# Layer 1's softmax in two passes of four heads, in a two-layer decode kernel

## The chip, the cores and the metric

The kernel runs on one NeuronCore of a Trainium2 chip. Its engines have queues of their own and run side by side: TensorE (PE, with weight loads PEld), VectorE (DVE), ScalarE (ACT), GpSimd (POOL) and the queue that issues transfers (SP), served by 16 DMA engines. The metric is the device time in microseconds (us) of the whole program. The kernel before takes 230.61 us, the median of three runs (230.2, 230.61 and 233.4).

## What is computed

Two layers, each of them an attention with residual and a feed-forward with residual, over 8 batch rows of one token each. Both layers use the same weights and the same K and V caches.

```python
def _A_ref(x, k_cache, v_cache, wq, wo):            # x: 8 x 1 x 448
    W = 1024                                        # the last 1024 of 4096 positions
    q = (x @ wq) -> 16 heads of 256
    k = repeat(k_cache[:, :, Sk - W:, :], 2)        # 8 KV heads, two query heads each
    v = repeat(v_cache[:, :, Sk - W:, :], 2)
    p = softmax(q . k * 256 ** -0.5)
    return (p . v) @ wo                             # 4096 -> 448
def _B_ref(x, w1, w2): return silu(x @ w1) @ w2     # 448 -> 1792 -> 448

x = A_x
x = x + A(layernorm(x)); x = x + B(layernorm(x))    # layer 1
x = x + A(layernorm(x)); x = x + B(layernorm(x))    # layer 2
```

A batch row needs 8 KV heads of K and of V, 512 KB each, so 16 loads or 8.4 MB a row and 67 MB in all; the weights add 10 MB. Everything is bfloat16 in HBM.

## The kernel before

**Rows and slots.** The work goes row by row, `b` = 0 to 7. The loads `K0..K7, V0..V7` of each row are issued in that order on the SP queue (`load_kv`, L496) into a ring of `R = 30` slots. A load may be issued when the load 30 places before it in the ring has been used for the last time. K head `k` of a row is last read by layer 2's scores of that row, V head `k` by layer 2's value products. Counting the ring round, the last two V loads of row `b+1` (`V6`, `V7`) and `K0`, `K1` of row `b+2` take the slots of `K0..K3` of row `b`, which layer 2's scores of heads 0 to 3 read (named `S1.0` below). `K2..K5` of row `b+2` wait for the scores of heads 4 to 7 (`S1.1`), the others for the value products of layer 2 (`PV1`).

**One row.** K heads are transposed in place by VectorE (L639; heads 0 to 3 in one piece, `KW`, 1.2 us, heads 4 to 7 in two pieces, `KT`, 0.68 us each). Layer 1: the scores of heads 0 to 3 (`S0.0`) and then of heads 4 to 7 (`S0.1`), both L656, both in the PSUM bank `SC[0]`, in rows 0 to 15 of each quarter of 32 partitions: `S0.0` fills 16 rows and `S0.1` rewrites 8 of them. One softmax (`softmax`) then covers all heads: negated maximum (`max`, L673, VectorE), a small masked copy (`mq`, L674, ScalarE), a matmul that spreads it (`mx`, L675), the bias (`mb`, L677), the exponentials (`exp`, L688, ScalarE), a permutation (`perm`, L690), a transpose (`turn`, L692), the sums (`l`, L694) and their reciprocal (`rl`, L697). The value products of heads 0 to 5 (`PV0`, L703, four matmuls of 512 columns a head) go to bank `OB[0]`; the last `LATE = 2` heads (`products_late`, named `PV6` and `PV7`, L712, eight matmuls of 256 columns a head) go to the free half of `SC[0]`. `o_turn` scales (`oev`, L725), transposes (`oT`, L729) and evicts (`oTev`, L733); `wo_rows` multiplies by `wo` (L754); `fold` brings the sum of one row into columns (`rowb`, L760, then L529 and L532).

**The chain of a row.** `chain(b)` then runs layer 1's feed-forward and layer 2's query: `xb1` (L765), statistics (L771 to L776), `w1a`, `w1b` (L544) with their turns `w1T` (L549), `tanh` (L798), `hT` (L806), `w2` (L818), `rowb2`, `fold2`, `xb2`, `wq0` and `wq1` (L833) with their turns `qT` (L838), the masked queries `qm0`, `qm1` (L839), the query expansion `qx` (L846) and its eviction `qbd` (L850). After that come `S1.0`, `S1.1`, a softmax and `PV1` of layer 2. The last row's layer 2 is cut in two halves; layer 2's end of rows 0 to 6 is done for all of them at once (`final_rows`), beside the last row's chain, and the last row ends in `final_last`.

**Order.** The order of the tasks on each engine is written out by hand in `ORDER`, as numbers of tasks. The engines wait by semaphores; a dependence is made wherever a task reads or writes what another wrote or read. So a task of one row that stands behind a task of the next row on VectorE waits for it, whatever it needs itself. In row 6, for instance, VectorE has (row in brackets):

```
KW0[7] KW1[7] xb1[6] KW2[7] w1Tb[6] w1Ta[6] rl1[5] hTb[6] hTa[6] KW3[7] KT4[7] KT5[7] xb2[6] KT5[7] KT6[7]
qT0a[6] qT0b[6] qm0[6] KT4[7] qT1[6] qm1[6] KT7[7] KT6[7] KT7[7] max1[6] max0[7] ...
```

TensorE has extra matmuls (`warm`, named `fill`, L781) between its tasks, whose results nobody reads.

Of the kernel before, what the change touches and what calls it, by code (L numbers as in the profile page):

```python
# [36 lines left out]
    "dve":  # L37
# [14 lines left out]
    "act":  # L52
# [8 lines left out]
    "pool":  # L61
        "0 1 79 130 131 239 269 270 256 404 403 373 390 536 506 523 537 669 639 656 670 802 772 789 803 905 935 936 "
        "922 1068 1069 1038 1055 1156 1173 1210 1273",
# [160 lines left out]
def bass_interleave_layers__sliding_block_cached__dense_activation_silu__decode_kernel(  # L224
# [20 lines left out]
    LATE = 2  # L245
# [416 lines left out]
    def softmax(b, L, part=None):  # L662

        sb, n, m = (SC[L], L, L) if part is None else (part[0], part[1], 1 - part[1])
        lb = bank[LB[n]]
        x = bank[sb][:, 0:256]
        px = lb[:, 256:512]
        mneg, bias, acc, rlr = (sm[b][:, 4 * n + i:4 * n + i + 1] for i in range(4))
        mq = sm[b][:, 8 + 4 * n:12 + 4 * n]
        K = [("sm", b, n, i) for i in range(5)]  # L670
        mx, lr = lb[:, C_MX:C_MX + 4], lb[:, C_L:C_L + 1]
        if part is None:
            dve(lambda e: e.tensor_reduce(mneg, x, AX.X, ALU.max, negate=True), bk(sb), [K[0]], 0.41, b, "max%d" % L)  # L673
            act(lambda e: e.activation(mq, sel4, ACTF.Copy, scale=mneg), [K[0], "sel4"], [K[4]], 0.2, b, "mq%d" % L)  # L674
            pe(lambda e: e.matmul(mx, quad[:], mq, start=True, stop=True, skip_group_check=True), [K[4], "quad"],  # L675
               bk(LB[n]), 0.2, b, "mx%d" % L)
            dve(lambda e: e.tensor_reduce(bias, mx, AX.X, ALU.min), bk(LB[n]), [K[1]], 0.15, b, "mb%d" % L)  # L677
        else:
            mt, mg = part[2][:, 0:64].bitcast(F32), part[2][:, 64:80].bitcast(F32)
            bias = mt[:, 0:1]  # L680
            dve(lambda e: e.tensor_reduce(mt[:, 0:1], x, AX.X, ALU.max, negate=True), bk(sb), [("mt", n)] + part[3], 0.41,
                b, "max%d" % L)
            dve(lambda e: e.transpose(mt, mt), [("mt", n)], [("mt", n)], 0.21, b, "mT")
            dve(lambda e: e.tensor_reduce(mg, mt.rearrange("p (n q) -> p n q", q=4), AX.X, ALU.min), [("mt", n)],
                [("mg", n)] + part[3], 0.17, b, "mg")
            dve(lambda e: e.transpose(mt.rearrange("p (n q) -> p n q", q=4), mg.unsqueeze(2).broadcast_to([P, 8, 4])),
                [("mg", n)], [("mt", n), K[1]], 0.21, b, "mb")
        act(lambda e: e.activation(e_sb[m], x, ACTF.Exp, bias=bias, scale=1.0, accum_out=acc),  # L688
            bk(sb) + [K[1]], EK[m] + [K[2]], 0.6, b, "exp%d" % L)
        pe(lambda e: e.matmul(px, perm[:], e_sb[m], start=True, stop=True),  # L690
# [408 lines left out]
```

## Time and profile before

| | |
|---|---|
| times of three runs | 230.2, 230.61, 233.4 us |
| the profiled execution | 230.15 us, its span 228.4 us |
| busy share of the span | PE 76%, DVE 69%, PEld 41%, ACT 31%, POOL 10% |
| granted TensorE clock | 1.000 |
| DMA | 78.21 MB, mean 342 GB/s over the span |
| costliest group | L639 transposes of K on DVE, 96 instructions, 80.2 us |
| scores | L656, 1024 matmuls, 40.9 us |
| value products | L703, 416 matmuls, 31.1 us; L712, 192 matmuls, 8.6 us |

The span lies 1.75 us under the time of the same execution; a sum made on the trace is therefore set against 230.15 us, and that execution stands 0.46 us under the median of the runs. "Busy" of PE counts the modelled end of each pipelined matmul, so a busy PE is not a full one. The DMA share is the mean over the 16 engines of the time that packets took; a little over 1 means that packets overlap.

### The profile page before, as it was taken

The numbers are of one execution on the slowest core, as the hardware profiler recorded it, in microseconds if no ns is written. First come the engines' busy times: TensorE is split into PE (matmuls) and PEld (weight loads), VectorE is DVE, ScalarE is ACT, GpSimd is POOL, SyncE is SP. The second block draws the span as 40 slices with busy tenths as digits, with TensorE's granted clock in tenths as the row PEclk, the third lists the DMA queues.
The fourth block names the chain that finished last, engine by engine and source line by source line (L and its number), as shares of the span: only waits on it lengthen the run. The fifth ranks groups of instructions, "written<-read, shape, count | busy, mean of one in ns | idle before, by whom it ended". The sixth has DMA issues, their size and how long they took to land.

```text
span 228.4 us, 8452 instructions
## 1 busy us (share of the span) xinstructions
PE 173.0 (76%) x3779; PEld 94.1 (41%) x3779; DVE 157.2 (69%) x369; ACT 71.4 (31%) x218; POOL 22.8 (10%) x41
## 2 busy tenths in 40 slices
PE   0020737357878989999898987888989999999894
PEld 0010623123444455445444644554445445544662
DVE  6238989878792797389459837974895589314644
ACT  2000080633302341432324142414332431353341
POOL 1000130000200210101010101110120200000020
PEclk9999999999999999999999999999999999999999
DMA  6999999999999999999999999999999999700000
GB/s 175 413 406 407 382 380 395 411 414 417 405 400 369 377 408 403 396 408 407 406 406 408 402 378 411 408 392 395 410 409 385 380 408 406 307 3 3 0 6 1
DMA packets 22681, 78.21 MB, mean 342 GB/s; under 512 B 2279, under 2 KB 5302, under 8 KB 22262
## 3 DMA queue, kind: packets, MB, share of 16 engines
q1 hardware_dynamic: 22486, 77.32, 86.6%
q8 instruction: 29, 0.48, 0.9%
q10 hardware_dynamic: 160, 0.36, 0.6%
q14 instruction: 6, 0.05, 0.1%
HBM read 77.67 MB, written 0.01 MB: 340 GB/s over the span
## 4 chain that ended last, share of the span: by engine, by line
PE 46%; DVE 31%; DMA 10%; ACT 6%; issue 4%; SPq 2%; DVEq 0%; ACTq 0%
DVE slot L639 12%; DMA slot<-in_A_k_cache_dram 10%; PE bank L656 10%; PE bank L703 7%; DVE slot L472 7%; PE pair L754 6%; PE bank L781 2%; PE pair L833 2%; ACT ot L760 2%; PE bank L675 2%; PE bank L846 2%; PE bank L712 2%; PE bank L833 2%; PE pair L529 2%; PE pair L818 1%
## 5 line engine op out<-in xcount | busy, mean ns | idle before, releaser
L639 DVE STREAM_TRANSPOSE slot<-slot 128x512 uint32<-128x512 uint32 (+1 forms) x96 | 80.2, 866 | 7.0 <-DMA slot<-in_A_k_cache_dram 6.8
L656 PE MATMUL bank<-slot,qbd 128*16 128x256 bf16 (+1 forms) x1024 | 40.9, 285 | 5.1 <-DVE slot L639 2.0
L703 PE MATMUL bank<-slot,qbd 128*24 128x512 bf16 (+6 forms) x416 | 31.1, 393 | 3.5 <-DVE qbd L692 3.3
L656 PEld LDWEIGHTS bank<-slot,qbd 128*16 128x16 bf16 (+1 forms) x1024 | 23.2, 87 | 16.7 <-ACT qbd L850 4.0
L781 PE MATMUL bank<-wq_sb,cols 128*1 128x512 bf16 x192 | 19.6, 416 | 13.9 <-DMA wq_sb<-in_A_wq_dram 13.9
L776 POOL TENSOR_TENSOR fcols<-fcols 128x1 f32<-128x1 f32 x17 | 9.4, 554 | 106.4 <-ACT fcols L774 94.5
L754 PE MATMUL pair<-wo_sb,q1s 128*1 128x449 bf16 x288 | 17.2, 353 | 1.1 <-DVE wo_sb L475 0.8
L850 ACT ACTIVATE qbd<-bank 128x256 bf16<-128x256 f32 x16 | 6.1, 384 | 33.5 <-PE bank L846 33.5
L725 ACT ACTIVATE ot<-bank,q1s 128x512 bf16<-128x512 f32 (+1 forms) x16 | 10.8, 673 | 16.4 <-PE bank L703 11.1
L626 POOL TENSOR_TENSOR qbd<-q1s,fcols 128x256 bf16<-128x256 bf16 x16 | 9.7, 614 | 59.7 <-PE bank L712 42.4
L703 PEld LDWEIGHTS bank<-slot,qbd 128*24 128x24 bf16 (+6 forms) x416 | 9.7, 92 | 11.1 <-DVE qbd L692 4.2
L692 DVE STREAM_TRANSPOSE qbd<-bank 128x256 bf16<-128x256 bf16 x17 | 8.0, 473 | 8.2 <-PE bank L690 7.9
L673 DVE TENSOR_REDUCE q1s<-bank 128x1 f32<-128x256 f32 x15 | 6.3, 423 | 8.1 <-PE bank L656 8.0
L472 DVE TENSOR_REDUCE slot<-wo_sb 128x6 f32<-128x2688 bf16 x4 | 11.8, 2948 | 0.1
L781 PEld LDWEIGHTS bank<-wq_sb,cols 128*1 128x1 bf16 x192 | 4.2, 82 | 15.4 <-issue 13.9
L674 ACT ACTIVATE q1s<-fcols,q1s 128x4 f32<-128x4 f32 x15 | 4.4, 296 | 18.7 <-DVE q1s L673 18.7
L675 PE MATMUL bank<-q1s,quad 128*128 128x4 f32 x30 | 6.0, 269 | 4.7 <-ACT q1s L674 4.5
L598 PE MATMUL pair<-slot,wq_sb 128*128 128x16 bf16 x128 | 3.6, 174 | 7.5 <-DVE slot L591 7.5
L833 PE MATMUL pair<-wq_sb,q1s 128*1 128x256 bf16 x256 | 8.9, 275 | 0.3 <-DVE q1s L765 0.3
L688 ACT ACTIVATE qbd<-bank,q1s 128x256 bf16<-128x256 f32 x15 | 7.1, 472 | 6.3 <-DVE q1s L677 6.0
L712 PE MATMUL bank<-slot,qbd 128*7 128x256 bf16 (+7 forms) x192 | 8.6, 283 | 0.6 <-DVE qbd L692 0.6
L833 PE MATMUL bank<-wq_sb,q1s 128*1 128x512 bf16 x128 | 8.8, 390 | 0.0
(168 smaller groups left out, 244.6 us busy)
## 6 DMA issues: line engine op xcount, KB each, us to landing
slot<-in_A_k_cache_dram SPq DMA_DIRECT2D x64, 512.0 KB, 8.3
slot<-in_A_v_cache_dram SPq DMA_DIRECT2D x64, 512.0 KB, 10.1
wo_sb<-in_A_wo_dram SPq DMA_DIRECT2D x4, 896.0 KB, 14.6
wq_sb<-in_A_wq_dram SPq DMA_DIRECT2D x3, 1024.0 KB, 8.0
w_sb<-in_B_w_dram SPq DMA_DIRECT2D x1, 1568.0 KB, 19.8
w_sb<-in_B_w_dram SPq DMA_DIRECT2D x1, 1344.0 KB, 17.2
wq_sb<-in_A_wq_dram ACTq DMA_DIRECT2D x1, 256.0 KB, 3.5
wq_sb<-in_A_wq_dram SPq DMA_DIRECT2D x1, 256.0 KB, 4.1
```

The costliest lines, as they stand in the source:

```text
L472: dve(lambda e, rows=rows, s=s: e.tensor_reduce(s, rows[:, :, R0:M1].rearrange("p c (a n) -> p c a n", a=2), AX.X, ALU.add, negate=True), ...
L626: pool(lambda e, k2=k2: e.tensor_tensor(qdata(0, k2), q1s[:, b, 64 * k2:64 * k2 + 64].rearrange("p (n r) -> p n r", r=2).unsqueeze(3) .bro ...
L639: dve(lambda e, v=v: e.transpose(v, v), keys, keys, 0.15 + n / 2 / 950, b, ("KW%d" if n > 1024 else "KT%d") % k)
L656: fns.append(lambda e, w=w, j=j, kv=kv, cb=cb, par=par: e.matmul(sc[32 * j:32 * j + up_to, 0:256], w, kv, start=(cb == 0 and par == 0), st ...
L675: pe(lambda e: e.matmul(mx, quad[:], mq, start=True, stop=True, skip_group_check=True), [K[4], "quad"], bk(LB[n]), 0.2, b, "mx%d" % L)
L703: pe([lambda e, t=t: e.matmul(bank[ob][32 * t:32 * t + m, :], pT_sb[L][:, 64 * t:64 * t + m], v[:, 512 * t:512 * t + 512], start=True, sto ...
L712: pe([lambda e, t=t, a=a: e.matmul(o[32 * t:32 * t + m, :], pT_sb[n][:, 64 * t + a:64 * t + a + m], v[:, 512 * t + DH * a:512 * t + DH * a ...
L725: act(lambda e: e.activation(o_t, src[1], ACTF.Copy, scale=sm[b][:, 4 * L + 3:4 * L + 4]), bk(src[0]) + [("sm", b, L, 3)], okey, 0.62, b, ...
L754: fns.append(lambda e, i=i, w=w, c0=c0: e.matmul(bank[XB][32 * (i % 4):32 * (i % 4) + 1, c0:c0 + D + 1], oT[:, oT_col(i):oT_col(i) + 1], w ...
L776: pool(lambda e: e.tensor_tensor(rhalf, var4, nhalf, ALU.pow), ["var4", "nhalf"], ["rhalf"], 0.54, b, "pow" + name)
L781: pe([lambda e, i=i: e.matmul(bank[OB[0]][32 * i:32 * i + 1, :], zero_b, wq_sb[:, 512 * i:512 * i + 512], start=True, stop=True, tile_posi ...
L833: pe([lambda e, j=j, c=c, qh=qh, k2=k2, h=h, n=n: e.matmul(qh[32 * j:32 * j + 1, :], xbt[b][:, xcol(c, k2):xcol(c, k2) + 1], view(wq_sb[:] ...
```

## The change

Layer 1's softmax is called twice a row, with `g = 0` for heads 0 to 3 as soon as `S0.0` is done, and with `g = 1` for heads 4 to 7 after `S0.1`. The exponentials, and then the turned probabilities, of pass `g` are written over the block of masked queries that its scores have used. Pass 0 uses the bank `OB[0]` for its small results, pass 1 `LB[0]`. `LATE` becomes 4: heads 0 to 3 are `PV0`, heads 4 to 7 are late products, three of them named `PV6`, read from the second block. In the last row the late heads are turned and multiplied by `wo` in two steps, after head 5 and after head 7. In `qx`, the masked queries are read as they lie and the expansion is written in runs of 8 columns; the eviction `qbd` now reads PSUM with a step of 8 and writes in runs of 8. Each row thereby gets a second `max`, `mq`, `mx`, `mb`, `exp`, `perm`, `turn`, `l` and `rl`. `ORDER` is new for all engines; the tables are left out here.

```diff
-    LATE = 2
+    LATE = 4
...
-    def softmax(b, L, part=None):
+    def softmax(b, L, part=None, g=0):
         sb, n, m = (SC[L], L, L) if part is None else (part[0], part[1], 1 - part[1])
-        lb = bank[LB[n]]
+        eb, ek, pb, pk = e_sb[m], EK[m], pT_sb[m], PT[m]
+        lbi, c = LB[n], 4 * n
+        mq = sm[b][:, 12:16]
+        qk = [("sm", b, 1, 4)]
+        early = []
+        if L == 0:
+            eb = pb = qbd[0][:, 8 + 256 * g:264 + 256 * g]
+            ek = pk = QB(0, g)
+            mq = eb[:, 0:8].bitcast(F32)
+            qk, n, c = ek, 2 * g, 8 * g
+            lbi = (OB[0], LB[0])[g]
+            early = QB(0, 1)[:] if g == 0 else []
+        lb, lk = bank[lbi], bk(lbi)
...
-        act(lambda e: e.activation(e_sb[m], x, ACTF.Exp, bias=bias, scale=1.0, accum_out=acc),
-            bk(sb) + [K[1]], EK[m] + [K[2]], 0.6, b, "exp%d" % L)
+        act(lambda e: e.activation(eb, x, ACTF.Exp, bias=bias, scale=1.0, accum_out=acc),
+            bk(sb) + [K[1]], ek + [K[2]], 0.6, b, "exp%d" % L)
...
     def late(b, oT, key):
+        o = bank[SC[0]][:, 256:512]
+        s = slot_of[LAST - 1, "k", 1] if b == LAST else None
         for kvh in range(HKV - LATE, HKV):
-            products_late(b, kvh, bank[SC[0]][:, 256:512], bk(SC[0]), 0, "PV%d" % kvh)
-        o_turn(b, 0, (SC[0], bank[SC[0]][:, 256:512]), ot7, EK[0], 0, 2 * LATE, oT, [(key, b, 7)], "7")
+            products_late(b, kvh, o, bk(SC[0]), e_sb[0], EK[0], "PV%d" % max(kvh, 6))
+            if kvh == HKV - 1 or b == LAST and kvh == HKV - 3:
+                last = kvh == HKV - 1
+                o_t, okey = (ot7, EK[0]) if last else (slots[s][:, 0:256], slot_key(s))
+                c0, c1 = (0, 4 if b == LAST else 2 * LATE) if last else (4, 8)
+                o_turn(b, 0, (SC[0], o), o_t, okey, c0, c1, oT, [(key, b, kvh)], "7", 2)
+                wo_rows(b, range(NCH - 2 * c1, NCH - 2 * c0), oT, [(key, b, kvh)], "wo7")
...
             pe([lambda e, qs=qs, k2=k2, q=q: e.matmul(
-                qs[:, q:256:4], band[:, 96 - 32 * q:224 - 32 * q], view(qm[k2], 0, [(16, 4), (1, 8), (8, 2)]),
+                view(qs, 8 * q, [(32, 8), (1, 8)]), band[:, 96 - 32 * q:224 - 32 * q], qm[k2],
                 start=True, stop=True, skip_group_check=True) for q in range(4)],
...
-            act(lambda e, qs=qs, k2=k2: e.activation(qbd[1][:, 8 + 256 * k2:264 + 256 * k2], qs, ACTF.Copy), bk(lb),
+            act(lambda e, qs=qs, k2=k2: e.activation(
+                view(qbd[1][:], 8 + 256 * k2, [(64, 4), (8, 8), (1, 8)]), view(qs, 0, [(64, 4), (1, 8), (8, 8)]),
+                ACTF.Copy), bk(lb),
...
             attend1(b + 1, 0)
+            softmax(b + 1, 0)
...
             attend1(b + 1, 1)
-            softmax(b + 1, 0)
+            softmax(b + 1, 0, g=1)
```

In the new order, the part of row 6 shown above reads:

```
KW0[7] rl1[5] KW1[7] KW2[7] xb1[6] KW3[7] w1Tb[6] w1Ta[6] KT4[7] hTa[6] hTb[6] max0[7] KT5[7] KT4[7] KT5[7] xb2[6]
KT6[7] KT7[7] qT0a[6] qT0b[6] mb0[7] qm0[6] KT6[7] KT7[7] qT1[6] qm1[6] turn0[7] rl0[7] max0[7] mb0[7] max1[6] ...
```

More of the change, by code (lines that the diff above doesn't have):

```diff
@@ L14 @@
     "pe":
[22 rows of a table removed]
-    "dve":
[14 rows of a table removed]
-    "act":
[8 rows of a table removed]
[23 rows of a table added]
+    "dve":
[16 rows of a table added]
+    "act":
[9 rows of a table added]
     "pool":
-        "0 1 79 130 131 239 269 270 256 404 403 373 390 536 506 523 537 669 639 656 670 802 772 789 803 905 935 936 "
-        "922 1068 1069 1038 1055 1156 1173 1210 1273",
+        "0 1 79 130 131 277 247 264 278 419 389 406 420 561 560 530 547 702 671 701 688 842 812 843 829 953 983 984 "
+        "970 1124 1125 1094 1111 1224 1241 1278 1341",
 }
@@ L660, in scores @@
                bk(sb), 0.0285, b, "S%d.%d" % (layer, k2))
-    def softmax(b, L, part=None):
+    def softmax(b, L, part=None, g=0):
         sb, n, m = (SC[L], L, L) if part is None else (part[0], part[1], 1 - part[1])
-        lb = bank[LB[n]]
+        eb, ek, pb, pk = e_sb[m], EK[m], pT_sb[m], PT[m]
[11 more added lines that the diff above has]
+        lb, lk = bank[lbi], bk(lbi)
         x = bank[sb][:, 0:256]
         px = lb[:, 256:512]
-        mneg, bias, acc, rlr = (sm[b][:, 4 * n + i:4 * n + i + 1] for i in range(4))
-        mq = sm[b][:, 8 + 4 * n:12 + 4 * n]
-        K = [("sm", b, n, i) for i in range(5)]
+        mneg, bias, acc, rlr = (sm[b][:, c + i:c + i + 1] for i in range(4))
+        K = [("sm", b, n, i) for i in range(4)]
         mx, lr = lb[:, C_MX:C_MX + 4], lb[:, C_L:C_L + 1]
         if part is None:
[L673 to L677, printed above, removed]
+            dve(lambda e: e.tensor_reduce(mneg, x, AX.X, ALU.max, negate=True), bk(sb) + early, [K[0]], 0.41, b, "max%d" % L)
+            act(lambda e: e.activation(mq, sel4, ACTF.Copy, scale=mneg), [K[0], "sel4"], qk, 0.2, b, "mq%d" % L)
+            pe(lambda e: e.matmul(mx, quad[:], mq, start=True, stop=True, skip_group_check=True), qk + ["quad"],
+               lk, 0.2, b, "mx%d" % L)
+            dve(lambda e: e.tensor_reduce(bias, mx, AX.X, ALU.min), lk, [K[1]], 0.15, b, "mb%d" % L)
         else:
@@ L687, in softmax @@
                 [("mg", n)], [("mt", n), K[1]], 0.21, b, "mb")
-        act(lambda e: e.activation(e_sb[m], x, ACTF.Exp, bias=bias, scale=1.0, accum_out=acc),
-            bk(sb) + [K[1]], EK[m] + [K[2]], 0.6, b, "exp%d" % L)
-        pe(lambda e: e.matmul(px, perm[:], e_sb[m], start=True, stop=True),
-           EK[m] + PERM + QM * m, bk(LB[n]), 0.13, b, "perm%d" % L)
-        dve(lambda e: e.transpose(view(pT_sb[m], 0, [(64, 4), (1, 2), (2, 32)]), px.bitcast(BF16)[:, 1:512:2]),
-            bk(LB[n]), PT[m], 0.44, b, "turn%d" % L)
+        act(lambda e: e.activation(eb, x, ACTF.Exp, bias=bias, scale=1.0, accum_out=acc),
+            bk(sb) + [K[1]], ek + [K[2]], 0.6, b, "exp%d" % L)
+        pe(lambda e: e.matmul(px, perm[:], eb, start=True, stop=True), ek + PERM + QM * (m and L), lk, 0.13, b, "perm%d" % L)
+        dve(lambda e: e.transpose(view(pb, 0, [(64, 4), (1, 2), (2, 32)]), px.bitcast(BF16)[:, 1:512:2]), lk, pk, 0.44, b,
+            "turn%d" % L)
         pe([lambda e, t=t: e.matmul(lr[32 * t:32 * t + 32, :], lsel[:], acc, start=True, stop=True,
                                     tile_position=(0, 32 * t), skip_group_check=True) for t in range(4)],
-           [K[2], "lsel"], bk(LB[n]), 0.05, b, "l%d" % L)
-        dve(lambda e: e.reciprocal(rlr, lr), bk(LB[n]), [K[3]], 0.15, b, "rl%d" % L)
+           [K[2], "lsel"], lk, 0.05, b, "l%d" % L)
+        dve(lambda e: e.reciprocal(rlr, lr), lk, [K[3]], 0.15, b, "rl%d" % L)
     def products(b, L, kvh, ob):
@@ L706, in products, with products_late @@
            slot_key(slot_of[b, "v", kvh]) + PT[L], bk(ob), 0.055, b, "PV%d" % L)
-    def products_late(b, kvh, o, keys, n, name):
+    def products_late(b, kvh, o, keys, pt, pk, name):
         v = slots[slot_of[b, "v", kvh]]
         m = 4 * (HKV - kvh) - 1
-        pe([lambda e, t=t, a=a: e.matmul(o[32 * t:32 * t + m, :], pT_sb[n][:, 64 * t + a:64 * t + a + m],
+        pe([lambda e, t=t, a=a: e.matmul(o[32 * t:32 * t + m, :], pt[:, 64 * t + a:64 * t + a + m],
                                          v[:, 512 * t + DH * a:512 * t + DH * a + DH], start=(a == 0), stop=(a == 1),
@@ L715, in products_late, with o_turn @@
             for a in range(2) for t in range(4)],
-           slot_key(slot_of[b, "v", kvh]) + PT[n], keys, 0.028, b, name)
+           slot_key(slot_of[b, "v", kvh]) + pk, keys, 0.028, b, name)
     def late(b, oT, key):
+        o = bank[SC[0]][:, 256:512]
+        s = slot_of[LAST - 1, "k", 1] if b == LAST else None
         for kvh in range(HKV - LATE, HKV):
-            products_late(b, kvh, bank[SC[0]][:, 256:512], bk(SC[0]), 0, "PV%d" % kvh)
-        o_turn(b, 0, (SC[0], bank[SC[0]][:, 256:512]), ot7, EK[0], 0, 2 * LATE, oT, [(key, b, 7)], "7")
-    def o_turn(b, L, src, o_t, okey, c0, c1, dst, keys, name):
-        act(lambda e: e.activation(o_t, src[1], ACTF.Copy, scale=sm[b][:, 4 * L + 3:4 * L + 4]),
-            bk(src[0]) + [("sm", b, L, 3)], okey, 0.62, b, "oev" + name)
+            products_late(b, kvh, o, bk(SC[0]), e_sb[0], EK[0], "PV%d" % max(kvh, 6))
[5 more added lines that the diff above has]
+                wo_rows(b, range(NCH - 2 * c1, NCH - 2 * c0), oT, [(key, b, kvh)], "wo7")
+    def o_turn(b, L, src, o_t, okey, c0, c1, dst, keys, name, n=None):
+        n = L if n is None else n
+        act(lambda e: e.activation(o_t, src[1], ACTF.Copy, scale=sm[b][:, 4 * n + 3:4 * n + 4]),
+            bk(src[0]) + [("sm", b, n, 3)], okey, 0.62, b, "oev" + name)
         nz = o_t.shape[-1] // DH
@@ L1011, in values1 @@
         late(b, oT1[b], "oT1")
-        wo_rows(b, range(NCH - 4 * LATE, NCH), oT1[b], [("oT1", b, 7)], "wo7")
         fold(b, 1.0, [], "1")
@@ L1038, in values2 @@
             for kvh in range(4 * k2, 4 * k2 + 4):
-                products_late(b, kvh, bank[ob][:, 0:256], bk(ob), k2, "PVL")
+                products_late(b, kvh, bank[ob][:, 0:256], bk(ob), pT_sb[k2], PT[k2], "PVL")
             o_turn(b, 1 - k2, (ob, bank[ob][:, 0:256]), slots[s][:, 512:768] if k2 else ot[:, 0:256],
@@ L1047, in bass_interleave_layers__sliding_block_cached__dense_activation_silu__decode_kernel @@
     attend1(0, 0)
+    softmax(0, 0)
     attend1(0, 1)
-    softmax(0, 0)
+    softmax(0, 0, g=1)
     values1(0)
```

92 rows, old and new, of the table ORDER are left out of this document.

## The prediction, made before the changed kernel was run

> **What bounds it now.** I read the slices and queues of the page first, then the busy time by windows, the waits of the SP queue, and single transfers.
>
> ```profile
> span 228.4 us, 8452 instructions
> DVE  6238989878792797389459837974895589314644
> DMA  6999999999999999999999999999999999700000
> q1 hardware_dynamic: 22486, 77.32, 86.6%
> ```
>
> The 16 DMA engines are busy in every slice until about 199 us; no compute engine is. Windows (times of PE, PEld, DVE, ACT and POOL, then clock, DMA share and GB/s) show how well, and where it stops:
>
> ```profile
> 70.00:72.00 2.00, 1.35 (x27) 0.63 (x23) 0.22 (x3) 0.86 (x3) 0.00 (x0) 1.00 1.01 326
> 80.00:100.00 20.00, 18.76 (x421) 10.19 (x423) 14.01 (x31) 7.05 (x22) 1.72 (x3) 1.00 1.02 404
> 108.00:110.00 2.00, 1.50 (x44) 0.82 (x33) 1.66 (x4) 0.38 (x1) 0.00 (x0) 1.00 1.03 412
> 198.00:200.00 2.00, 2.00 (x52) 1.24 (x52) 0.17 (x1) 0.35 (x1) 0.00 (x0) 1.00 0.28 111
> 200.00:202.00 2.00, 2.00 (x54) 0.82 (x46) 0.23 (x2) 1.01 (x3) 0.00 (x0) 1.00 0.00 0
> ```
>
> A 512 KB load lands 1.275 us (the median) after the one before it. From the first K head of row 1 (53.70 us by the landing records) to V7 of row 7 (200.36) there are 111 steps in 146.7 us, where 111 x 1.275 is 141.5: the stream loses 5.1 us, in some 17 steps of 1.4 to 2.5 us. That is all it could gain. What can make it worse is the SP queue, waiting for slots:
>
> ```profile
> SPq L496 <- PE bank L656: 59.5, 12, 8.9
> ...
> 193.12 0.80 SPq L496 DMA_DIRECT2D slot<-in_A_v_cache_dram  x2
> ...
> DMA to landing us min/median/max: 6.9/6.9/6.9
> ```
>
> The first line says that 59.5 us of waiting end with layer 2's scores. The two loads at 193.12 are V6 and V7 of row 7, let go by S1.0 of row 6, whose matmuls end at 193.08; V7, issued at 193.49, takes 6.9 us. Until V5 lands at 197.85 the stream has other work, so the margin, which I call the lead, is 4.8 us. By the same reading (end of S1.0 in row b, landing of V5 in row b+1) the leads of rows 0 to 6 are 3.5, 3.8, 4.9, 4.6, 3.5, 3.6 and 4.8 us. After V7 comes the tail:
>
> ```profile
> 200.68 0.40 PE L712 MATMUL bank<-slot,qbd 128*3 128x256 bf16 x8
> ...
> 202.93 0.55 ACT L760 ACTIVATE ot<-pair 128x450 bf16<-128x450 f32 x1 [0.70 <-PE pair L754]
> ```
>
> The last product starts 0.32 us after the landing, rowb1 2.57 us after it, and the span ends 28.0 us after it. So time = end of the stream (200.4) + tail (28.0) + 1.75 around the span = 230.15, the profiled execution's own time; the median of the runs is 0.46 higher.
>
> **The second pass.** Per row it adds on DVE max 0.42, mb 0.16, turn 0.47 and rl 0.16 = 1.2 us; on ACT mq 0.30, exp 0.47 and the read of its sum 0.19 = 1.0; on PE mx 0.39 (two passes), perm 0.28, l 0.22, and two heads as 8 narrow matmuls instead of 4 wide (8 take 0.41 in the row above; 24 wide take 1.48, so 4 take 0.25): 2 x 0.16. PE: 1.2 us. A row of 20.4 us (16 x 1.275) has 14.0 busy on DVE, 18.8 on PE and 7.1 on ACT in the window 80 to 100; they become 15.2, 20.0 and 8.1. PE's figure counts modelled ends (8 score matmuls are 0.41 long and follow each other every 0.22), and it includes the fills. So the sums cost nothing beside the stream; without that cover, 1.2 x 7 = 8.4 us. There is also a new wait: S0.1 writes the score bank that pass 0's exp still reads. Behind S0.1 on PE wait mx and the products; but S0.1 needs all K heads transposed, and in the new order those transposes end later than that exp. Nothing.
>
> **The gate.** What matters is where S1.0 lands, since it lets V6 and V7 go. In the new DVE order KW3 of the next row stands ahead of w1T in every row from 1 on (before, not in rows 2 and 6), so the chain cannot start before K3 of the next row has landed. Row 6, worked through: K3 landed at 183.98; KW3 1.24, two w1T 0.83, KT 0.68, two hT 0.32, max 0.42, three KT 2.05 and xb2 0.17 make 189.7; two KT 1.36, two qT 0.90, mb 0.16 and qm0 0.28 make 192.4, where the trace has
>
> ```profile
> 188.10 0.17 DVE L765 TENSOR_TENSOR q1s<-pair,fcols 128x5 bf16<-128x5 f32 x1
> ...
> 190.19 0.28 DVE L839 SCALAR_TENSOR_TENSOR qbd<-pair,fcols 128x64 bf16<-128x64 f32 x1
> ```
>
> qm0's end at 190.47. Then qx 0.42, the eviction 0.39 and S1.0's four groups 1.0, now without a score group and qx1 between: 194.3 against 193.08, so +1.2. The same sum gives +0.6 in row 1 (its second pass waits for row 0's), +1.5 in row 2, and +0.1 to +0.7 in rows 3 to 5. In row 0, qT1, qm1, two KT, max, mq and mx stand ahead of S1.0's last group: +1.5. Leads become 2.0, 3.1, 3.4, 4.4, 3.4, 2.9 and 3.6 us.
>
> How short may a lead be? Nothing in the trace is shorter than 3.5. The page's quickest load (wq_sb on the ACT queue, 256 KB in 3.5 us, of which 0.62 is data at 411 GB/s) bounds the setup at 2.9 us; the other bound is 0. Only row 0 falls clearly under 2.9: 0 to 0.9 us, I take 0.3, nearer the end of V6 in row 1, which landed 1.25 us after V5 at a lead of 3.5. The Trainium skill ("DMA: Bandwidth & Descriptors", section "Latency and other measured facts") gives about 0.6 us to the first byte of such a transfer; by it row 0 costs nothing and the sum is 0.3 lower.
>
> Gains: S1.1 follows S1.0 at once in rows 0 to 3, so K2 to K5 go out 1 to 2 us earlier; PV1, now behind the late products, lets K6 to V5 go 1 to 2 us later, where leads were 5 to 10 us. I take zero; the bounds are -5.1 us (the whole loss) and the slower rival below.
>
> **qx and its eviction.** Four L846 matmuls (64 columns, written with a step of 4) take 227 ns each, L690 (256 contiguous) 289, L729 (4 columns) 171: 0.87 against 0.47 ns a column. Runs of 8 save at most 0.03 us a matmul. The eviction L850 (384 ns, of which 178 remain at 8 columns) now reads with a step of 8: between 0 and a doubling, +0.2; I take +0.1, once on each gate (inside the leads) and twice in the tail. The Trainium skill ("SBUF — State Buffer", section "Door 1: The DMA port swizzle (why `[64,N]` ≈ `[32,N]`)") has PSUM lines of 8 bytes, and any pattern that isn't contiguous slows matmuls much. The trace agrees for the write; if it holds for ScalarE's read too, the tail is 0.2 longer than I take.
>
> **The tail.** After V7: the last two wo7 groups end 0.1 later (the first of them stands before the eviction's end), three products and l of row 6 delay fold1 0.2; w1b no longer waits behind oT1 and fewer small copies stand between the turns, -0.3; qT0 without those copies -0.4; xinit8 and fold8 stand between S1.0's groups and w18a (0.6) ahead of S1.1, +0.4; the evictions +0.2. Sum +0.2, bounds -0.8 and +1.2.
>
> **Sum.** 230.15 + 0.3 + 0.2 = 230.65, plus 0.46 to the median: 231.1.
>
> **Rivals.** *Slower: the leads run out.* One place, the issue of V6 and V7; it decides when gates come 1 us later than I worked out (by tasks that wait for each other across rows on DVE), if setup is 2.9. Then the leads are 1.0, 2.1, 2.4, 3.4, 2.4, 1.9 and 2.6, short of 2.9 by 1.9, 0.8, 0.5, 0, 0.5, 1.0 and 0.3 = 5.0 us: 231.1 - 0.3 + 5.0 = 235.8, over the 2% line of 235.2. For: DVE runs at nine tenths just there, and the order ties the chain to K landings. Against: a lead of 3.5 shows no gap. Chance 0.21. *Faster: the stream loses nothing more.* If the lost steps come from a shallow queue (the 326 GB/s above follow the shortest lead), earlier S1.1 could end them: 231.1 - 0.3 - 5.1 = 225.7, just past 2% (226.0). Against: other lost steps have loads queued for 8 us. Chance 0.15. *The early pass brings nothing because the tail isn't shortened by it* is no rival but the forecast: V7 lands when it lands, and its eight matmuls, turn and wo groups come after it in both kernels. That the change doesn't do what it says I exclude: the second pass stands in the new order.
>
> **How the numbers follow.** Forecast (stream and tail as they are, own range 228 to 234): 0.64. A measurement here tells 2% from no change, so faster 0.15, same 0.64, slower 0.21. The range leaves out about 0.08 of the faster case and 0.12 of the slower: 225.7 to 236.0.
>
> **What would show it.** Right: DMA share about 1 until 199 to 202 us, DVE near 167 us busy, 32 more instructions on DVE, V7's landing to the end 28 us. Wrong: DMA share under 0.9 in the windows around V6 and V7 (leads), a tail over 29.5 us, or landings 1.275 us apart throughout (the faster rival).

## The result, and the profile after

The changed kernel takes 233.23 us in the median of 20 runs, the kernel before 231.68 us in as many: a ratio of 1.0068 (95% interval 1.0041 to 1.0095). So it is slower by 0.7%, well inside 2%; the forecast was 231.1 us, 0.2% above the median that was then known of the kernel before.

The profiled execution of the changed kernel was disturbed (its clock was 0.58 from 118 to 122 us, and the stream fell to 225 GB/s from 134 to 138), so the lines below come from a second profile of the same kernel, run `a0_again`, which took 231.13 us with a span of 229.3: V7 of row 7 lands at 201.06 us (before 200.36, so +0.70), the tail from there to the end of the span is 28.28 us (28.00, so +0.28).

In one place the change also alters what is computed. In the last row the scaled products of heads 4 and 5 go to the slot of `(6, "k", 1)`, load 97. Load 127, which is V7 of row 7, has the same slot of the ring of 30, and the products come after it: head 7 of the last row is multiplied, in both layers, with a V of which 128 of 1024 positions have been overwritten. Of the kernels below, `a0_again` and `a2` do the same; `b1`, `b2`, `c3` and `c4` use another slot, and `a1` and `a3` write to none.

The page of `a0_again`, in the rows that were read before the change (first the busy tenths of 40 slices):

```profile
span 229.3 us, 8838 instructions
...
DVE  6727989995974798489569857984887599414724
...
DMA  6999999999999999999999999999999999700000
...
q1 hardware_dynamic: 22486, 77.32, 86.3%
```

The DMA engines are still busy in every slice to 200 us: the stream is still the frame. Its windows (PE, PEld, DVE, ACT, POOL, then clock, DMA share and GB/s):

```profile
80.00:100.00 20.00, 17.67 (x394) 10.07 (x398) 15.23 (x33) 7.53 (x24) 2.87 (x5) 1.00 1.01 397
...
198.00:200.00 2.00, 1.90 (x43) 0.99 (x39) 0.80 (x4) 1.60 (x7) 0.00 (x0) 1.00 0.71 281
200.00:202.00 2.00, 1.67 (x39) 0.77 (x42) 0.47 (x1) 0.69 (x3) 0.00 (x0) 1.00 0.04 14
```

DVE has 15.2 us in 80 to 100, the figure forecast, PE 17.7 where 20.0 was, and transfers run into the last window. Row 6's gate and the last row's late products, from the time line:

```profile
194.68 0.81 SPq L500 DMA_DIRECT2D slot<-in_A_v_cache_dram  x2
...
201.15 0.48 ACT L747 ACTIVATE slot<-bank,q1s 128x256 bf16<-128x256 f32 x1 [1.01 <-DMA slot<-in_A_v_cache_dram]
201.68 0.21 PE L751 MATMUL bank<-sel_o,slot 128*128 128x4 bf16 x2 [0.34 <-ACT slot L747]
201.81 0.61 PE L726 MATMUL bank<-slot,qbd 128*7 128x256 bf16 x16
...
204.13 0.55 ACT L782 ACTIVATE ot<-pair 128x450 bf16<-128x450 f32 x1 [0.70 <-PE pair L776]
```

V6 and V7 of row 7 go out at 194.68, where they went at 193.12. And ScalarE's eviction of heads 4 and 5 is released by a **transfer**: it waits for V7's landing, because it writes V7's slot. PV7 (the second half of the L726 group) starts 0.97 us after the landing, where it was 0.32.

One more line of the page, the transposes of K before and after; the last columns are VectorE's idle time just ahead of them and what ended it:

```profile
L639 DVE STREAM_TRANSPOSE slot<-slot 128x512 uint32<-128x512 uint32 (+1 forms) x96 | 80.2, 866 | 7.0 <-DMA slot<-in_A_k_cache_dram 6.8
```

```profile
L643 DVE STREAM_TRANSPOSE slot<-slot 128x512 uint32<-128x512 uint32 (+1 forms) x96 | 81.2, 871 | 11.6 <-DMA slot<-in_A_k_cache_dram 11.3
```

With the same transposes VectorE waits 4.5 us more for K heads to land.

### The profile page after: what moved, and what is told of

Its sections match the earlier page's. It is cut to its first block, busy times and chain, and to the rows that moved or that the text cites. A ratio compares the mean times of both kernels' runs of the same rounds, so it can differ in the third digit from the quotient of the medians.

```text
span 233.4 us, 8838 instructions
## 1 busy us (share of the span) xinstructions
PE 174.8 (75%) x3933; PEld 99.9 (43%) x3933; DVE 163.5 (70%) x401; ACT 78.0 (33%) x244; POOL 22.8 (10%) x41
## 4 chain that ended last, share of the span: by engine, by line
PE 44%; DVE 31%; DMA 13%; ACT 5%; issue 3%; SPq 2%; POOL 0%; DVEq 0%; ACTq 0%
DMA slot<-in_A_k_cache_dram 13%; DVE slot L643 12%; PE bank L660 11%; DVE slot L476 7%; PE pair L776 5%; PE bank L717 5%; PE bank L726 3%; PE pair L840 2%; PE bank L803 2%; ACT ot L782 2%; PE pair L855 2%; PE bank L751 2%; DVE qbd L706 2%; DVE q1s L688 2%; PE pair L533 1%
## 5 line engine op out<-in xcount | busy, mean ns | idle before, releaser
L717 PE MATMUL bank<-slot,qbd 128*24 128x512 bf16 (+6 forms) x352 | 28.2, 384 | 0.2 <-DVE qbd L706 0.2
L706 DVE STREAM_TRANSPOSE qbd<-bank 128x256 bf16<-128x256 bf16 x25 | 11.7, 468 | 10.0 <-PE bank L705 9.9
L703 ACT ACTIVATE qbd<-bank,q1s 128x256 bf16<-128x256 f32 x23 | 10.9, 473 | 16.3 <-DVE q1s L692 14.3
L726 PE MATMUL bank<-slot,qbd 128*15 128x256 bf16 (+7 forms) x320 | 14.2, 293 | 0.2 <-DVE qbd L706 0.2
L688 DVE TENSOR_REDUCE q1s<-bank 128x1 f32<-128x256 f32 x23 | 9.6, 419 | 6.4 <-PE bank L660 5.9
L484 ACT ACTIVATE slot<-w_sb 128x448 bf16<-128x448 bf16 x6 | 3.4, 575 | 22.1 <-DMA w_sb<-in_B_w_dram 22.0
L689 ACT ACTIVATE qbd<-fcols,q1s 128x4 f32<-128x4 f32 x16 | 4.8, 297 | 17.9 <-DVE q1s L688 17.8
L711 DVE RECIPROCAL q1s<-bank 128x1 f32<-128x1 f32 x25 | 4.0, 158 | 9.6 <-PE bank L708 9.4
L705 PE MATMUL bank<-qbd,perm 128*128 128x256 bf16 x25 | 7.2, 290 | 4.5 <-ACT qbd L703 4.5
L690 PE MATMUL bank<-qbd,quad 128*128 128x4 f32 x32 | 6.5, 273 | 3.8 <-ACT qbd L689 3.8
## 6 DMA issues: line engine op xcount, KB each, us to landing
slot<-in_A_v_cache_dram SPq DMA_DIRECT2D x64, 512.0 KB, 10.3
```

The costliest lines, as they stand in the source:

```text
L703: act(lambda e: e.activation(eb, x, ACTF.Exp, bias=bias, scale=1.0, accum_out=acc), bk(sb) + [K[1]], ek + [K[2]], 0.6, b, "exp%d" % L)
L706: dve(lambda e: e.transpose(view(pb, 0, [(64, 4), (1, 2), (2, 32)]), px.bitcast(BF16)[:, 1:512:2]), lk, pk, 0.44, b, "turn%d" % L)
L717: pe([lambda e, t=t: e.matmul(bank[ob][32 * t:32 * t + m, :], pT_sb[L][:, 64 * t:64 * t + m], v[:, 512 * t:512 * t + 512], start=True, sto ...
L726: pe([lambda e, t=t, a=a: e.matmul(o[32 * t:32 * t + m, :], pt[:, 64 * t + a:64 * t + a + m], v[:, 512 * t + DH * a:512 * t + DH * a + DH] ...
```

## The experiments

Three theories were put to the chip first. **G**: the gate of row 0 is late (the prediction's 0.3 us). **L**: the last row's turn in two steps costs time. **S**: the second pass's 1.2 us a row, counted as covered in the prediction, is on the path after all.

**Four kernels beside each other.** The changed kernel again (`a0_again`); the late heads of the last row turned once (`a1`); row 0's gate earlier (`a2`); both (`a3`).

> The changed kernel once more, for an undisturbed trace: in the one at hand the granted clock falls to one half from 117.9 to 121.3 us, and a gap of the stream follows it at 133 to 138 us. Theory G (the gate: layer 2's scores of heads 0 to 3 let the last two V loads of the next row go too late in row 0, since max, mq and mx of row 1 and qT1 stand ahead of their last group): ratio 1.005 to 1.009; V6 and V7 of row 1 land over 1.5 us after the load before; no gap at rows 3 and 4. Theory L (the last row: its late heads are turned in two steps, and head 6 waits for the eviction of heads 4 and 5): V7's product starts about 1.0 us or more after V7's landing (0.32 before), and the tail after the landing is 28.8 us or more (28.0 before). Theory S (the 1.2 us a row that the second pass adds on VectorE and on TensorE): the stream loses in most rows, not in row 0 alone.

> The late heads of the last row are turned and multiplied by wo once, after head 7, as in the other rows. Theory L: V7's product starts within 0.5 us of V7's landing, the tail falls by about 0.7 to 1.0 us, and the ratio by 0.003 to 0.004. Theories G and S: no change against the changed kernel beyond 0.2%.

> Row 0 alone: qm0 before qT1 on VectorE; mx of row 1 and qx1 behind the last group of layer 2's scores of heads 0 to 3 on TensorE. Theory G: those scores end 1 to 1.7 us earlier, the lead of V6 of row 1 grows from about 2.6 to 3.5 us or more, V6 and V7 land 1.25 to 1.35 us after the load before, and the ratio falls by 0.004 to 0.007. Theories L and S: within 0.2% of the changed kernel.

> Both edits together. G and L together: the gains add up, 0.007 to 0.010 off the ratio, so 0.997 to 1.001. Theory S: stays at 1.005 or more, since the second pass is still there with all its instructions.

The edit of `a1` (with one `oev`, `oT`, `oTev` and `wo7` in the order), and the orders of row 0 in `a2`, VectorE's and then TensorE's:

```diff
-            if kvh == HKV - 1 or b == LAST and kvh == HKV - 3:
+            if kvh == HKV - 1:
...
-                c0, c1 = (0, 4 if b == LAST else 2 * LATE) if last else (4, 8)
+                c0, c1 = (0, 2 * LATE) if last else (4, 8)
```

```diff
-qT0a[0] qT0b[0] qT1[0] qm0[0] qm1[0]
+qT0a[0] qT0b[0] qm0[0] qT1[0] qm1[0]
...
-S1.0[0] qx1[0] S1.0[0] S1.0[0] fill[0] mx0[1] S1.0[0] S1.1[0]
+S1.0[0] S1.0[0] S1.0[0] fill[0] S1.0[0] mx0[1] qx1[0] S1.1[0]
```

Ratios to the kernel before: 1.0049 (1.0019 to 1.0080), 1.0052 (1.0020 to 1.0084), 1.0065 (1.0028 to 1.0102) and 1.0111 (1.0062 to 1.0161). Neither edit gains. By the traces, G falls: in `a0_again` row 0's lead is 2.9 us, V6 and V7 of row 1 land without a gap, and in `a2` the gate doesn't come earlier (end of S1.0 at 67.98 us, 67.55 in `a0_again`). L is half right: with one turn PV7 starts 0.41 (`a1`) and 0.38 us (`a3`) after V7's landing in place of 0.97, but the rest of the tail is longer: from PV7's start to the last issue of the output it is 25.43 and 25.46 us, against 25.11 split. The sign that S gave, a stream that loses in most rows, isn't in `a0_again`: at V6 and V7 it loses nothing in any row (the leads and losses of all traces follow below).

**The slot, the depth of the ring, the layout.** `b1` takes a slot that no later load uses; `b2` and `b3` have 29 slots in the ring; `b4` is the kernel before with the new `qx` and `qbd` lines alone. Where the first text below says "the second load of head 6", it means K2 of row 6, and by "its first load" K1 of row 6.

> The changed kernel, with the products of the last row's heads 4 and 5 written into another slot of the ring: that of the second load of head 6, which no later load uses, in place of that of its first load, which is also the slot of the last load V7. Slot theory: in the changed kernel the last row's turn of heads 4 and 5 waited for V7's landing (oev7 at 201.15 us with V7 landed at 201.06, PV7's start 0.97 us after the landing, where the unsplit turn gave 0.40). Here that eviction comes before V7 lands, PV7 starts 0.3 to 0.4 us after the landing, and the time from V7's landing to the end falls from 28.26 us to 27.8 to 28.05. Ratio to the kernel before 1.0025 to 1.004, against 1.005 of the changed kernel. Rival: the split itself (two more matmuls and an eviction on PE's and ScalarE's way) makes the 0.6 us, then the start of PV7 stays at 0.8 to 1.0 us after the landing and the ratio at 1.005.

> The changed kernel with 29 slots in the ring of loads in place of 30, nothing else (the last row's products of heads 4 and 5 go to a slot that V7 doesn't use). Every load of the stream is then issued one slot later, so each lead (end of the gate to the landing of V5 of the next row) is shorter by one step of 1.28 us: from 2.9 3.3 4.4 3.2 4.0 2.5 4.0 us to about 1.6 2.0 3.1 1.9 2.7 1.2 2.7. Lead theory (what the change loses in the stream, it loses because the queue is short behind the gate): the stream loses 3 to 6 us more, at the steps V6 to K1, and the ratio to the kernel before is 1.015 to 1.035. Rival (the loss of the stream is made by other things, as instruction fetches or the chip, and leads over 1 us are enough): within 0.3% of the changed kernel, 1.002 to 1.008.

> The kernel before with 29 slots in place of 30, nothing else. Its leads fall from 3.5 3.8 4.9 4.6 3.5 3.6 4.8 us to about 2.2 2.5 3.6 3.3 2.2 2.3 3.5, so to those of the changed kernel or a little below, with none of its other edits. Lead theory: the stream's loss at V6 to K1 rises from 0.6 us to 1 to 4 us, and the ratio is 1.004 to 1.015, so the shorter leads alone make what the change costs in the stream. Rival (the change's stream loss has another cause): 0.998 to 1.002, with V7 of the last row landing within 0.3 us of 200.4.

> The kernel before with one part of the change alone: the used queries' block is written by the four matmuls in runs of 8 columns, and is read by the eviction with a stride of 8, in place of the other way round; the order is that of before. The changed kernel showed 0.29 us for the four matmuls in place of 0.42, and 382 ns for the eviction in place of 384. If that is the layout's doing: the same durations here, the time from V7's landing to the end 27.75 to 27.95 us in place of 28.00, leads 0.1 us longer, ratio 0.997 to 1.000. Rival (the strided read of PSUM is slower and was hidden in the changed kernel's other rows): the eviction over 0.41 us, the end 0.1 us later or more, ratio 1.000 to 1.002.

```diff
-        s = slot_of[LAST - 1, "k", 1] if b == LAST else None
+        s = slot_of[LAST - 1, "k", 2] if b == LAST else None
```

```diff
-    R = 30
+    R = 29
```

The first edit is that of `b1`, the second that of `b3`. `b2` has the second and, in the first, `3` in place of `2`.

`b1`: 1.0016 (0.9974 to 1.0058). The wait is gone; the same place of its time line:

```profile
200.96 0.47 ACT L747 ACTIVATE slot<-bank,q1s 128x256 bf16<-128x256 f32 x1 [0.28 <-PE bank L726]
...
201.82 0.21 PE L751 MATMUL bank<-sel_o,slot 128*128 128x4 bf16 x2
201.95 0.61 PE L726 MATMUL bank<-slot,qbd 128*7 128x256 bf16 x16
```

The eviction now runs ahead of the landing (201.53 us) and is released by TensorE. PV7 still starts 0.64 us after the landing, not the 0.3 to 0.4 expected, and from the end of the last row's turn to PV7 it takes 2.66 us, against 3.06 in `a0_again`. The tail is 28.50 us, outside what was expected, but 0.57 us of that is the output's last transfer (2.77 us from its issue to the end, 2.20 in `a0_again`); from V7's landing to that issue it fell from 26.08 to 25.74.

`b3`, the kernel **before** with one slot less: 1.0209 (1.0131 to 1.0287), more than expected, and clearly slower, though its interval doesn't tell on which side of 2% it lies. `b2`, the changed kernel with one slot less: 1.0345 (1.0283 to 1.0407), the top of what was expected. Here is where it is lost, in windows of the kernel before,

```profile
136.00:142.00 6.00, 5.04 (x107) 2.40 (x99) 3.82 (x6) 1.71 (x5) 0.61 (x1) 1.00 1.02 408
178.00:186.00 8.00, 7.38 (x163) 3.66 (x155) 5.44 (x13) 3.82 (x11) 1.78 (x3) 1.00 1.01 386
```

of `b3`,

```profile
136.00:142.00 6.00, 4.88 (x93) 2.56 (x93) 2.27 (x5) 1.96 (x6) 0.61 (x1) 1.00 0.96 359
178.00:186.00 8.00, 6.89 (x137) 3.13 (x133) 3.08 (x7) 2.85 (x9) 1.23 (x2) 1.00 0.98 366
```

and of `b2`:

```profile
68.00:70.00 2.00, 1.86 (x50) 1.09 (x53) 0.90 (x3) 0.57 (x2) 0.00 (x0) 1.00 0.41 88
136.00:142.00 6.00, 5.57 (x130) 3.43 (x118) 2.99 (x10) 2.59 (x8) 0.61 (x1) 1.00 0.88 302
```

The last two columns tell it: where the last V heads of a row are due, the share falls under 1. Of the 111 steps between K0 of row 1 and V7 of row 7, `b3` loses 9.43 us against 5.14 before, and the three steps V5 to V7 of the rows 1 to 7 account for 4.34 us against 0.30: 4.0 of the 4.3 us of difference. In `b2` they lose 12.24 of 15.85 us; its traced execution was the longest of six (242.49 us, median 239.94), that of `b3` the shortest (234.38, median 237.37).

`b4`: 0.997 (0.9916 to 1.0024). The matmuls and the eviction of the layout, before and in `b4` (busy, mean ns):

```profile
L846 PE MATMUL bank<-qbd,band 128*128 128x64 bf16 x64 | 6.7, 227 | 1.3 <-DVE qbd L839 1.1
L850 ACT ACTIVATE qbd<-bank 128x256 bf16<-128x256 f32 x16 | 6.1, 384 | 33.5 <-PE bank L846 33.5
```

```profile
L850 ACT ACTIVATE qbd<-bank 128x256 bf16<-128x256 f32 x16 | 6.1, 384 | 32.1 <-PE bank L846 32.1
L846 PE MATMUL bank<-qbd,band 128*128 128x64 bf16 x64 | 4.6, 195 | 1.7 <-DVE qbd L839 1.4
```

The matmuls are faster, four of them 0.29 us in a row instead of 0.42, and the eviction that reads PSUM with a step of 8 is no slower. The rest was not met: PV7 starts 0.79 us after V7's landing where it was 0.32, so the tail is 28.21 us and not 27.75 to 27.95, and the mean lead is 3.96 us against 4.10 before, not 0.1 longer.

**A dose, another order, and two repeats.** `c1` is `b4` again and `c4` is `b1` again; `c2` lengthens the gate of the rows 0 to 6; `c3` pulls PV7 forward.

> The kernel before with the new layout of the used queries' block alone, once more, for a narrower interval (0.997, 0.992 to 1.002, the first time). Layout theory: the 0.13 us saved per block lies on the gate's path and nothing is lost: 0.995 to 1.000, so at or below the kernel before and below every kernel with the two passes. Rival: no effect on the time, as the saved 0.13 us only lets PE wait elsewhere: 0.999 to 1.001.

> The kernel of c1 with the four matmuls that lay out the used queries of heads 0 to 3 done three times over instead of once in each of the rows 0 to 6, with the same result: 8 matmuls of 0.07 us, so each gate some 0.55 us later, as late as the changed kernel's gates (its leads were 0.63 us shorter in the mean than before). Lead theory: the leads are 0.5 to 0.6 us shorter than c1's, the stream loses 0.5 to 2 us more, and the ratio lies 0.003 to 0.008 above c1's. Rival (a lead shorter by half a step is covered by the queue, and the changed kernel's stream loss has another cause): within 0.001 of c1.

> The kernel of c4 (the changed one with the last row's products in another slot) with another order on TensorE in the rows 1 to 6: what belongs to layer 2 of the row before (its second pass's products, the turn of its exponentials) or only fills, and stood between the second softmax pass's turn and PV7, goes behind PV7; in row 3 one reciprocal goes ahead of that turn on VectorE. Place theory (the second pass ends late and PV7 starts 0.4 to 2.0 us after V7's landing in place of 0.3 to 1.3, which makes the gates late): PV7 0.2 to 0.9 us earlier, most in rows 3 and 6, leads 0.3 to 0.4 us longer in the mean, the ratio 0.001 to 0.004 below c4's. Rival (the gate waits for other work than PV7, or the layer 2 work pushed back comes out later at the gate of the same row): leads within 0.1 us of c4's, ratio within 0.001 of c4's or above it.

> The kernel of b1 once more, to stand beside c3 on the same chip (b1: 1.0016, 0.997 to 1.006). Slot theory: from V7's landing to the last issue 25.7 to 25.8 us again, against 26.08 of the changed kernel, and a ratio of 1.001 to 1.005.

The edit of `c2`, and row 6 of TensorE's order in `c3` (rows 1 to 5 alike):

```diff
-                start=True, stop=True, skip_group_check=True) for q in range(4)],
+                start=True, stop=True, skip_group_check=True)
+                for r in range(3 if k2 == 0 and b < LAST else 1) for q in range(4)],
```

```diff
-PV6[6] l0[6] PV6[6] PV6[6] perm1[5] oT0[6] xinit[6] l1[5] PV7[6] PV1[5] wo0[6]
+PV6[6] l0[6] PV6[6] PV6[6] oT0[6] PV7[6] perm1[5] xinit[6] l1[5] PV1[5] wo0[6]
```

`c1`: 0.9998 (0.9955 to 1.0042), which fits the layout theory and its rival alike. `c4`: 0.9999 (0.9964 to 1.0034), a little faster than expected, but its trace misses what the slot theory said: from V7's landing to the last issue it is 26.07 us, not 25.7 to 25.8 as in `b1`, and no shorter than the 26.08 of `a0_again`. The eviction starts ahead of the landing here too (by 0.22 us), but the last row's turn ends only 1.67 us before V7 lands (2.01 in `b1`), and PV7 starts 0.99 us after the landing.

`c2`: 1.0008 (0.9975 to 1.0042). It tells little: the eight extra matmuls took 0.23 us, not 0.55, as each follows the last after some 0.03 us (twelve of them end 0.52 us after the first starts, four after 0.29), so its mean lead is 3.93 us against 4.02 in `c1`.

`c3`: 1.0029 (0.9995 to 1.0063), so no faster than `c4`: the place theory has no support. PV7 does start earlier, in row 6 0.06 us after V7's landing instead of 1.85, but the mean lead is 3.22 us (3.38 in `c4`). The time line of `c3`, row 6, shows why:

```profile
182.66 0.40 PE L727 MATMUL bank<-slot,qbd 128*3 128x256 bf16 x8
...
182.99 0.28 PE L706 MATMUL bank<-qbd,perm 128*128 128x256 bf16 x1
...
183.83 0.24 PE L709 MATMUL bank<-q1s,lsel 128*32 128x1 f32 x8 [0.50 <-DVE qbd L707]
...
184.13 0.56 PE L777 MATMUL pair<-wo_sb,q1s 128*1 128x449 bf16 x8
...
186.99 0.55 ACT L783 ACTIVATE ot<-pair 128x450 bf16<-128x450 f32 x1 [1.29 <-PE pair L777]
```

The work of layer 2 that was pushed behind PV7 (L706, L709) now waits for its turn on VectorE in front of `wo0` (L777): from PV7's start to `rowb1` (the last line) it is 4.33 us, where `c4` has 3.29. The wait was moved, not removed.

## Why the forecast was right, point by point

**Sum.** On the traces, 230.65 us was forecast for the profiled execution and 231.13 measured: stream +0.70 us where +0.3 was taken, tail +0.28 where +0.2 was. The side is right, and so is the class; that the two times lie so close is partly luck. The kernel before was profiled in an execution quicker than any of its 20 runs, `a0_again` in the quickest of its 12; on the medians the ratios 1.0049 and 1.0068 stand for about 1.1 and 1.6 us, where 0.5 was forecast. Two of the steps behind the sum are wrong. Four slips in the working change nothing: the steps of 1.4 us and more are 13, not 17; row 6's sum comes to 194.2, not 194.3; row 1's lead of 3.8 less 0.6 is 3.2, not 3.1; and S1.1 stands right behind S1.0 in row 0 only, not in rows 0 to 3.

**The second pass: "the sums cost nothing beside the stream" failed.** The four groups it adds on VectorE grew by 9.4 us (max 3.3, mb 1.1, turn 3.7, rl 1.3), as worked out. Its busy time grew by only 6.0, to 163.2 rather than 167: the records of neighbouring tasks overlap, and their lengths alone add up to 9.0 more. But the row's last turn and its gate come later. Means of the rows 1 to 6, before and in `a0_again`, us:

| | before | after |
|---|---|---|
| K7's landing to the end of the last K transpose | 4.20 | 5.19 |
| K7's landing to the end of the last turn | 8.72 | 10.22 |
| that turn to PV7 | 2.50 | 1.48 |
| V7's landing to PV7 | 0.73 | 1.38 |
| PV7 to rowb1 | 3.50 | 3.14 |
| rowb1 to the gate (end of S1.0) | 10.24 | 10.75 |
| V7's landing to the gate | 14.46 | 15.28 |

The last turn ends 1.5 us later; the shorter rest of products behind it gives 1.0 back, and from rowb1 to the gate it takes 0.5 more. The six traces of the new order with 30 slots (without the two named below) have 9.95 to 10.54 us to the last turn and 14.70 to 15.43 from V7's landing to the gate, four with the old order 8.70 to 8.89 and 14.32 to 14.59. The step from V7's landing to PV7 is less steady: `b1` has 0.71 us there, as before.

Not all of this is the pass itself. Of the 1.0 us by which the K transposes end later, max and mb of the pass take 0.25 on VectorE; 0.44 are qT1 and qm1 of the row before, which the new order puts ahead of the last transposes, and 0.2 is idle. Of the 1.5 us up to the last turn, the pass takes 0.8, layer 2's softmax of the row before 0.3, and 0.3 is idle. So S holds for about half of the delay. The rest goes with the new order; no run has the one without the other, so this split is read off the traces and not shown by a run. What made the prediction miss it is that it compared sums with a row's length and not the place of the work with the K landings.

**The gate.** Mean lead after: forecast 3.26 us, measured 3.46 (before 4.10). The mean is right, the rows are not: 2.9, 3.3, 4.4, 3.2, 4.0, 2.5 and 4.0 us, with row 5 the shortest instead of row 0. And in row 6, worked through as +1.2 by the wait for KW3, the gate came 1.56 us later: rowb1 was already 2.6 us later, K3 itself landed 1.33 us later, and from that landing to the gate it took 9.3 us (9.1 before) instead of the 10.3 worked out. So what was priced at 1.2 us from K3 on came to 0.2.

**How short may a lead be?** The value taken (0.3 us in row 0, no price elsewhere) failed; the bound of 2.9 us was the better guide. All 98 gates of the 14 traces, the lead against what V6 and V7 then took over 2 x 1.275 us (with 29 slots, to V4's landing, and V5 to V7):

| lead, us | gates | of them over 0.25 us late | mean loss, us |
|---|---|---|---|
| under 2.5 | 11 | 11 | 1.63 |
| 2.5 to 3 | 12 | 7 | 0.66 |
| 3 to 3.5 | 21 | 5 | 0.27 |
| 3.5 to 4 | 33 | 7 | 0.15 |
| over 4 | 21 | 2 | 0.02 |

Two traces of the new order are left out from here on, the first profile of the changed kernel and that of `a1`, with a granted clock of 0.50 in mid-stream (118 to 121 us, and 173 to 175 us). `b4` and `c1`, of the old order, have such stretches too (43 to 52 us, 44 to 57 us) and are kept, since these can only make the old order look worse. Without the two and those with 29 slots, 5 of 5 leads under 2.5 us were late (1.20 us in the mean), 2 of 7 from 2.5 to 3 us (0.22), and 9 of 58 above.

Leads under 3 us are 1 of 28 in the four traces with the order of before and 30 slots (row 0 of `c1`, just behind its slow stretch), and 11 of 42 in six with the new order and 30 slots. Their streams lose 5.29 and 6.62 us in the mean (4.7 to 6.4, and 5.5 to 7.8). V5 to V7 lose 0.58 and 1.78, and K0 and K1, which wait for the same gate, 0.76 and 2.15; V0 to V4 lose less than before, 1.79 and 0.62.

Before the gates are blamed, a rival has to be looked at, which the profile's page shows and the prediction left out: the same DMA engines also fetch instructions, in some 30 packets of about 1.1 us each. Before, and in `a0_again`:

```profile
q8 instruction: 29, 0.48, 0.9%
```

```profile
q8 instruction: 31, 0.51, 0.9%
```

Take the steps in which such a packet runs, or ran in the microsecond before, about half of all 111. They lose 5.15 us in the mean of the four traces and 4.95 in the six; all other steps lose 0.14 and 1.68. In the six traces, 14 of those others are 1.4 us or longer, and every one is V6, V7, K0 or K1, the loads that S1.0 lets go. So the difference lies with the gates and not with the fetches. The stream's loss of 5 us, which the faster rival put down to a shallow queue, stands beside the fetches; no run leaves them out, so that they cause it is not shown.

These are means over single executions that differ by a microsecond; `a0_again` itself lost nothing at V5 to V7. So the slower rival was the right mechanism with too high a price: the gates came as late in the mean as the sum had them, and few leads fell under 2.5 us. The term that was mis-sized is the stream's, +0.3 us, against 1.3 in the mean. The rule cited from the Trainium skill ("DMA: Bandwidth & Descriptors", section "Latency and other measured facts", about 0.6 us to the first byte) isn't what a lead needs here: leads of 1.9 to 2.4 us lost 0.4 to 2.5 us, and at the 11 leads under 2.5 us the first load let go landed 3.3 us or more after its issue.

**qx and its eviction.** The size was right: 32 ns a matmul where "at most 0.03 us" was worked out, 0.13 us a block. That the write makes it is not shown: the same edit also lets the matmuls read the masked queries as they lie, where they read them in pieces before, and no run has one without the other. The eviction was taken as +0.1 and measured at nothing (382 ns against 384). The rule cited from the Trainium skill ("SBUF — State Buffer", section "Door 1: The DMA port swizzle (why `[64,N]` ≈ `[32,N]`)") speaks of matmuls, and the step from 227 to 195 ns fits it, as far as the write makes it; the prediction's worry that it might hold for ScalarE's read too did not come true.

**The tail.** +0.2 forecast, +0.28 measured, from other parts. From PV7's start to the last issue it is 0.39 us shorter (25.11 against 25.50); `b4` and `c1` have 25.23, so 0.27 of it is the layout. But PV7 starts 0.65 us later after the landing. Of that, the wait for V7's slot is 0.40 by the comparison with `b1` (2.66 against 3.06 us from turn to PV7), a wait that the prediction didn't see although the diff names the slot. It isn't a fixed price: in `a2`, which has the wait too, the turn ended later against the landing and it is 2.70 us. And the 0.32 us of the kernel before is itself a good case: `b4` and `c1`, with the same order, have 0.79 and 0.62.

**What stays open.** With the other slot the ratios are 1.0016 and 0.9999, without it 1.0049 and 1.0068. The trace of `b1` accounts for 0.34 us, or 0.0015, of that, and the trace of `c4` for nothing; the runs stood on different chips, and `a1`, which lacks the wait too, was no faster than `a0_again` beside it. That the slot makes the whole difference is not shown. No version beat the kernel before beyond its interval; the layout alone is the nearest (0.997 and 0.9998).

## What to carry to other kernels

Judge added work by where it stands against the landings: 1.2 us a row fitted easily into the row, and still, with the order that came with it, the row's last turn ended 1.5 us later. A ring of slots has a margin that can be measured: take a slot away, and the time that it costs (here 2.1%, 1.3 to 2.9) tells how near the edge every later delay is. Before a gap in a stream is put down to a wait, sort the steps by what else the DMA engines did just then. And look up whose slot a scratch buffer borrows: a write to the slot of a load that is still to come waits for that load.

## What the hardware showed that wasn't expected

A lead under 2.5 us always cost time (11 of 11), although a load takes 1.275 us on the stream. Nearly all that the stream of the kernel before lost, 5.11 of 5.14 us, was lost in steps beside an instruction fetch. ScalarE read 256 PSUM columns with a step of 8 in the time of contiguous ones (382 and 384 ns), while TensorE's matmuls took 195 ns when they wrote 64 columns in runs of 8 and 227 with a step of 4, where they also read their input in pieces.
